# The end of a decode kernel: the last eleven rows of w4 summed on four column groups, the final copy divided between two engines, the output issued by SyncE

## Chip, cores, metric

One core of a Trainium2 chip. The metric is device time in microseconds (us). Each run also has a span, from the first to the last instruction of the program in the record (rounded to 0.1 us), and a granted TensorE clock. Ratios are the mean time of one kernel's fast runs over that of the other's fast runs of the same rounds, so they are not quite the ratio of the medians that are quoted.

## The reference, cut to what matters

```python
xn = layernorm(x)                                    # one token, D = 1024
out = x + attention(layernorm-ed x) @ wo + mixer_mlp(xn)
# attention: 32 query heads, 4 KV heads, 65536 keys of 128: 134 MB of K and V
# mixer_mlp ends in gelu(layernorm(x1) @ w3) @ w4,   w4: 3584 x 1024 (7.3 MB)
# output: 1 x 1 x 1024, bf16
```

About 170 MB pass through the core once, and the result is one row.

## The kernel before

SyncE issues all large loads in one order into three slots of SBUF: wq, w3, w1 and w2, then K and V in 8 MB blocks, wo, and last w4. w4 comes in eight pieces, smaller towards the end, so that little work follows the last byte. The row `psB` in PSUM gathers everything that is added to the output. It lies as two halves of 512 columns on partitions 0 and 32, two column groups of TensorE (matmuls that `tile_position` places so that group j writes from partition 32j on).

```python
W4_PIECES = (6, 5, 6, 4, 3, 2, 1, 1)          # 28 rows of w4

def row_acc(j, lhsT, rhs, start=False):
    nc.tensor.matmul(psB[32 * j:32 * j + lhsT.shape[1], :], lhsT=lhsT, rhs=rhs, start=start, stop=False,
                     tile_position=(0, 32 * j), skip_group_check=True)
# ... cut ...
def compute_w4(lo, hi):
    wt = st.tiles["w4"]
    for c in range(lo, hi):
        for j in range(2):
            row_acc(j, hT[:, c:c + 1], wt[:, D * c + 512 * j:D * c + 512 * (j + 1)])
# ... cut ...
early = sum(W4_PIECES[:2])
compute_w4(0, early)
project(HKV - 1)
compute_w4(early, FC)
out_t = ogpool.tile([64, 512], BF16, name="out_t", tag="og")
nc.scalar.copy(out=out_t[:], in_=psB[0:64, :])
nc.scalar.dma_start(out=out[0, 0, :].rearrange("(j n) -> j n", j=2),
                    in_=out_t[:].rearrange("(a b) n -> a b n", b=32)[:, 0, :])
```

## Time and profile before

402.85 us, median of three runs (402.81 to 403.03).

| part of the end, from the timeline and the chain | us |
|---|---|
| last row of w4 has landed | 397.32 |
| its two matmuls | 397.36, 0.40 long |
| ScalarE copies 64x512 out of PSUM | 397.78, 0.58 long |
| ScalarE's sequencer (the part of an engine that waits and issues DMAs) issues the output DMA | 398.39, 0.58 long |
| end of the span | 400.91 |

Two lines of the page of the kernel before, in 40 equal slices of the span: the busy share of the DMA engines in tenths, and what they moved.

```profile
DMA  9989999999999999999999999999999999999895
GB/s 412 425 366 433 451 425 425 503 425 418 414 419 432 418 497 420 425 418 425 432 433 471 425 425 418 433 432 432 464 420 425 418 445 394 428 481 432 380 418 205
```

The loads never pause until the last slice. So only what follows the last landed byte can be made shorter by a change at the end. The chain that ended last, before (start in us, length in us, what):

```profile
379.92 17.40 DMA big<-in_B_w_dram
397.32 0.04 issue
397.36 0.40 PE psB L179 x2
397.76 0.02 issue
397.78 0.58 ACT out_t L443
```

The timeline of the same stretch (start, length, engine, line, operation; in brackets the idle time and what ended it):

```profile
392.91 1.03 PE L179 MATMUL psB<-big,hT 128*1 128x512 bf16 x8 [0.16 <-DMA big<-in_B_w_dram]
394.81 0.81 PE L179 MATMUL psB<-big,hT 128*1 128x512 bf16 x6 [0.87 <-DMA big<-in_B_w_dram]
397.36 0.38 PE L179 MATMUL psB<-big,hT 128*1 128x512 bf16 x2 [0.26 <-DMA big<-in_B_w_dram]
397.78 0.58 ACT L443 CAST out_t<-psB 64x512 bf16<-64x512 f32 x1 [29.53 <-PE psB L179]
398.39 0.58 ACTq L444 DMA_DIRECT2D out_dram<-out_t  x1
```

TensorE waits for each piece of w4 in turn: it has time to spare until the last one. After the last landing at 397.32 there are 3.59 us in a row without overlap (400.906 - 397.317).

### The profile page before, as it was taken

The numbers are of one execution on the slowest core, as the hardware profiler recorded it, in microseconds if no ns is written. First come the engines' busy times: TensorE is split into PE (matmuls) and PEld (weight loads), VectorE is DVE, ScalarE is ACT, GpSimd is POOL, SyncE is SP. The second block draws the span as 40 slices with busy tenths as digits, with TensorE's granted clock in tenths as the row PEclk, the third lists the DMA queues.
The fourth block names the chain that finished last, engine by engine and source line by source line (L and its number), as shares of the span: only waits on it lengthen the run. The fifth ranks groups of instructions, "written<-read, shape, count | busy, mean of one in ns | idle before, by whom it ended". The sixth has DMA issues, their size and how long they took to land.

```text
span 400.9 us, 2563 instructions
## 1 busy us (share of the span) xinstructions
PE 230.4 (57%) x1348; PEld 44.2 (11%) x854; DVE 209.0 (52%) x154; ACT 27.3 (7%) x35; POOL 5.3 (1%) x28
## 2 busy tenths in 40 slices
PE   0470970591668246922965195629453936594985
PEld 0210000010200110010102010201020002000231
DVE  0511010974196549644953894269349931975040
ACT  1001010003000200020002000100100020002000
POOL 2000000000000000000000000000000000000000
PEclk9995795597679666968796799568866986697999
DMA  9989999999999999999999999999999999999895
GB/s 412 425 366 433 451 425 425 503 425 418 414 419 432 418 497 420 425 418 425 432 433 471 425 425 418 433 432 432 464 420 425 418 445 394 428 481 432 380 418 205
DMA packets 4575, 170.01 MB, mean 424 GB/s; under 512 B 467, under 2 KB 469, under 8 KB 982
## 3 DMA queue, kind: packets, MB, share of 16 engines
q1 hardware_dynamic: 4560, 169.87, 98.4%
q8 instruction: 8, 0.13, 0.1%
q14 instruction: 1, 0.01, 0.0%
q10 hardware_dynamic: 6, 0.00, 0.0%
HBM read 169.87 MB, written 0.00 MB: 424 GB/s over the span
## 4 chain that ended last, share of the span: by engine, by line
DMA 52%; DVE 26%; PE 16%; ACT 3%; another core or an unknown queue 2%; issue 1%; DVEq 0%; ACTq 0%
DMA big<-in_A_k_cache_dram 31%; DVE big L315 19%; DMA big<-in_A_v_cache_dram 10%; PE sc L320 8%; PE oacc L370 6%; DMA big<-in_A_wq_dram 6%; DMA big<-in_B_w_dram 4%; DVE p_sb L341 3%; DVE mx L325 3%; ACT p_sb L338 3%; PE psq L245 1%; PE pm_mx L327 0%; DVE m L329 0%; PE pm_mx L334 0%
## 5 line engine op out<-in xcount | busy, mean ns | idle before, releaser
L320 PE MATMUL sc<-big,qdiag 128*128 128x512 bf16 x512 | 127.7, 409 | 66.4 <-DVE big L315 66.4
L315 DVE STREAM_TRANSPOSE big<-big 128x4096 f32<-128x4096 f32 x32 | 139.4, 4413 | 50.5 <-DMA big<-in_A_k_cache_dram 50.4
L370 PE MATMUL oacc<-big,p_sb 128*32 128x512 bf16 x512 | 44.7, 521 | 34.5 <-DVE p_sb L341 34.5
L325 DVE TENSOR_REDUCE mx<-sc 128x1 f32<-128x2048 f32 x8 | 18.3, 2292 | 29.8 <-PE sc L320 29.8
L320 PEld LDWEIGHTS <-qdiag 128*128 128x128 bf16 x128 | 13.0, 102 | 176.6 <-issue 145.9
L338 ACT ACTIVATE p_sb<-sc,nball 128x2048 bf16<-128x2048 f32 x8 | 15.7, 1967 | 218.7 <-DVE nball L336 218.7
L341 DVE STREAM_TRANSPOSE p_sb<-p_sb 128x2048 bf16<-128x2048 bf16 x8 | 18.5, 2311 | 18.0 <-ACT p_sb L338 18.0
L370 PEld LDWEIGHTS <-p_sb 128*32 128x32 bf16 x512 | 16.6, 126 | 59.4 <-DVE p_sb L341 35.1
L245 PE MATMUL psh<-big,ln_rep_b 128*32 128x512 bf16 (+1 forms) x64 | 12.4, 941 | 8.0 <-DMA big<-in_B_w_dram 8.0
L409 PE MATMUL o_acc<-big,oT 128*1 128x512 bf16 x48 | 12.5, 428 | 2.4 <-ACT p_sb L338 2.4
L327 PE MATMUL pm_mx<-ident_f,mx 128*1 128x128 f32 x8 | 2.3, 283 | 19.1 <-DVE mx L325 19.1
L284 DVE STREAM_TRANSPOSE h_row<-h_row 128x896 bf16<-128x896 bf16 x1 | 1.1, 1111 | 21.1 <-ACT h_row L283 21.1
L379 DVE SCALAR_TENSOR_TENSOR og<-oacc,wb,og 128x512 f32<-128x512 f32 x4 | 3.0, 745 | 15.7 <-PE oacc L370 15.7
L179 PE MATMUL psB<-big,hT 128*1 128x512 bf16 x56 | 7.4, 378 | 1.8 <-DMA big<-in_B_w_dram 1.7
L193 PE MATMUL pm_ln<-ln_rowsum_a,ones_f 128*128 128x1 f32 x2 | 0.6, 347 | 13.3 <-DVE ln_rowsum_a L191 13.3
L415 DVE COPY o_rows<-o_acc 1x1024 f32<-1x1024 f32 x1 | 1.2, 1212 | 13.3 <-PE oacc L370 13.3
L184 DVE STREAM_TRANSPOSE x_t<-x_row 32x256 bf16<-32x256 bf16 x4 | 2.5, 616 | 8.9 <-DMA x_row<-in_A_x_dram 8.9
L269 POOL COPY qdiag<-qx 32x32 bf16<-32x32 bf16 x16 | 3.2, 203 | 279.9 <-PE sc L320 249.7
L391 PE MATMUL pm_e<-ol,sel8big 128*128 128x129 f32 x8 | 2.3, 370 | 8.2 <-DVE ol L390 8.2
L245 PE MATMUL psq<-big,ln_rep_a 128*32 128x512 bf16 x64 | 5.9, 547 | 1.3 <-DMA big<-in_A_wq_dram 1.3
L257 DVE CAST q_row<-psq 128x512 bf16<-128x512 f32 x1 | 0.7, 691 | 7.9 <-PE psq L245 7.9
L334 PE MATMUL pm_mx<-ident_f,rep 1*128 1x1 f32 x8 | 1.9, 241 | 5.0 <-DVE rep L331 5.0
(95 smaller groups left out, 72.6 us busy)
## 6 DMA issues: line engine op xcount, KB each, us to landing
big<-in_A_wo_dram SPq DMA_DIRECT2D x1, 8192.0 KB, 36.7
big<-in_B_w_dram SPq DMA_DIRECT2D x1, 7168.0 KB, 38.5
big<-in_B_w_dram SPq DMA_DIRECT2D x2, 2048.0 KB, 46.4
big<-in_B_w_dram SPq DMA_DIRECT2D x2, 1536.0 KB, 27.3
big<-in_B_w_dram SPq DMA_DIRECT2D x1, 1280.0 KB, 24.1
big<-in_B_w_dram SPq DMA_DIRECT2D x1, 1024.0 KB
big<-in_B_w_dram SPq DMA_DIRECT2D x1, 768.0 KB, 30.8
big<-in_B_w_dram SPq DMA_DIRECT2D x1, 512.0 KB, 31.5
```

The source lines that it names most:

```text
L179: nc.tensor.matmul(psB[32 * j:32 * j + lhsT.shape[1], :], lhsT=lhsT, rhs=rhs, start=start, stop=False, tile_position=(0, 32 * j), skip_gro ...
L184: nc.vector.transpose(out=x_t[32 * a:32 * a + 32].rearrange("p c j -> p (c j)"), in_=x_row[:, 256 * a:256 * (a + 1)].rearrange("p (i c) -> ...
L245: nc.tensor.matmul(acc[32 * q:32 * q + 32, i, 0:n], lhsT=rep[:, c, :], rhs=cols(c, i, q), start=(c == 0), stop=(c == DC - 1), tile_positio ...
L269: nc.gpsimd.tensor_copy(out=qdiag[at, LEAD:].rearrange("p (x c) -> p x c", x=4)[:, :, 32 * a:32 * a + 8], in_=qx[at, :, 8 * g:8 * g + 8])
L315: nc.vector.transpose(out=words, in_=words)
L320: nc.tensor.matmul(sc[:, e, :], lhsT=qdiag[:, c0:c0 + P], rhs=cols[:, s, e, :, b2, :, r], start=(s == 0 and b2 == 0 and r == 0), stop=(s = ...
L325: nc.vector.reduce_max(out=mx[:], in_=sc[:].rearrange("p e n -> p (e n)"), axis=AX.X)
L338: nc.scalar.activation(out=p_sb[:], in_=sc[:], func=ACTF.Exp, bias=nball[:, b:b + 1], scale=SCALE, accum_out=group["lall"][:, b:b + 1])
L341: nc.vector.transpose(out=flat, in_=flat)
L370: nc.tensor.matmul(oacc[32 * q:32 * (q + 1), :], lhsT=pT[:, e, 32 * t:32 * (t + 1)], rhs=vt[:, :, e, t, :], start=(e == 0 and t < 4), stop ...
L379: nc.vector.scalar_tensor_tensor(out=og[:], in0=oacc[:], scalar=wb[:, 1:2], in1=og[:], op0=ALU.mult, op1=ALU.add)
L409: nc.tensor.matmul(tail["rows"][0:1, h2, :], lhsT=oT[g][:, j:j + 1], rhs=wt[:, g, j, 512 * h2:512 * (h2 + 1)], start=(g == 0 and j == 0), ...
```

## The change

The intent is to shorten that row of steps. From row 17 on, w4 is summed on four column groups of 256 columns, in a second PSUM bank. What stood in `psB` by then is folded into it once by matmuls with the identity. The final copy has 256 columns instead of 512 and is shared by ScalarE and VectorE, and SyncE, which has nothing left to do, issues the output.

```diff
+    def compute_w4_quarters(lo, hi, start=False):
+        wt = st.tiles["w4"]
+        for c in range(lo, hi):
+            for q in range(4):
+                nc.tensor.matmul(tail["quarters"][32 * q:32 * q + 1, :], lhsT=hT[:, c:c + 1],
+                                 rhs=wt[:, D * c + 256 * q:D * c + 256 * (q + 1)], start=(start and c == lo),
+                                 stop=(c == FC - 1), tile_position=(0, 32 * q), skip_group_check=True)
+
+    def fold_halves():
+        halves = ppool.tile([64, 512], F32, name="halves", tag="p")
+        nc.vector.tensor_copy(out=halves[:], in_=psB[0:64, :])
+        for q in range(4):
+            j, h = divmod(q, 2)
+            nc.tensor.matmul(tail["quarters"][32 * q:32 * q + 32, :], lhsT=ident_f[0:64, 32 * j:32 * j + 32],
+                             rhs=halves[:, 256 * h:256 * (h + 1)], start=True, stop=False,
+                             tile_position=(0, 32 * q), skip_group_check=True)
 ... cut ...
+    tail["quarters"] = ps_M.tile([P, 256], F32, name="quarters", tag="pm")
     early = sum(W4_PIECES[:2])
+    halved = sum(W4_PIECES[:3])
     compute_w4(0, early)
     project(HKV - 1)
-    compute_w4(early, FC)
-    out_t = ogpool.tile([64, 512], BF16, name="out_t", tag="og")
-    nc.scalar.copy(out=out_t[:], in_=psB[0:64, :])
-    nc.scalar.dma_start(out=out[0, 0, :].rearrange("(j n) -> j n", j=2),
-                        in_=out_t[:].rearrange("(a b) n -> a b n", b=32)[:, 0, :])
+    compute_w4(early, halved)
+    fold_halves()
+    compute_w4_quarters(halved, FC)
+    out_t = ogpool.tile([P, 256], BF16, name="out_t", tag="og")
+    nc.scalar.copy(out=out_t[:, 0:128], in_=tail["quarters"][:, 0:128])
+    nc.vector.tensor_copy(out=out_t[:, 128:256], in_=tail["quarters"][:, 128:256])
+    nc.sync.dma_start(out=out[0, 0, :].rearrange("(j n) -> j n", j=4),
+                      in_=out_t[:].rearrange("(a b) n -> a b n", b=32)[:, 0, :])
```

## The prediction

> **What bounds the kernel now.** The load stream: the page's slices show the DMA engines at 90% or more nearly everywhere, about 424 GB/s, and the chain of waits ends in the w4 load for 17.4 us. Only what follows w4's last byte can be shortened here. By the chain and the timeline of the end (profile span 400.9 us): the last w4 row lands at 397.32; its two 512-column matmuls start at 397.36 and take 0.40 together; the ScalarE copy 64x512 starts at 397.78 and takes 0.58; the ACT-issued output DMA starts at 398.39 and takes 0.58, to 398.97; about 1.9 us of landing and program end follow. So 3.6 us is exposed; 1.6 us of it is touched.
>
> **What changes, costed.**
> 1. Last row: four 256-column matmuls on four column groups instead of two of 512. A 512-column one takes 378 ns, 213 of it streaming at full clock; I estimate 272 ns for 256, with starts some 10 ns apart (three weight loads here overlap within 0.09 us). About 0.31 instead of 0.40: saves 0.09.
> 2. Copies: the ScalarE forms (1014 ns at 1024 columns, 597 at 512, 484 at 384) give about 0.27 us for 128 columns; VectorE's cast from PSUM of the same 128x128 shape takes 0.293. Side by side this would save 0.29. But in the built kernel the VectorE copy waits on ScalarE, not on the matmuls, so I expect them one after the other: 0.27 + 0.04 + 0.29 = 0.60; no saving, 0.02 to 0.05 lost. It fits the Trainium skill, "PSUM — Partial Sum Buffer", section "PSUM bank collisions raise a hardware error": two engines on one bank and quadrant collide, reads against reads too, and both halves lie in one bank. The trace before has no such pair to confirm it.
> 3. Output issue: SyncE's issues take 0.33 to 0.52 us, ACT's 0.52 and 0.58. I take 0.42 for a small one: saves about 0.15. The extra cross-engine hand-over costs 0.02 to 0.05. Landing should not change: the skill's "DMA: Bandwidth & Descriptors", section "Issuing engines are not separate DMA queues", says the issuer saves sequencer time only.
> 4. Added: a VectorE copy 64x512 (0.69 by the like cast) and four fp32 fold matmuls (about 0.6, from the 585 ns passes of the o_rows matmuls, overlapped over column groups) after row 16, about 392.75 to 394.1. Rows 17 to 20 landed at 392.9, so PE falls behind by 1.2 us; at 0.11 to 0.23 us a row it is back before rows 24 and 25 land at 396.07. Off the critical path, with 0.3 us or more to spare.
>
> **On the critical path:** -0.09 (matmuls), +0.03 (copies), -0.15 (issue): about -0.2 us.
>
> **Predicted time: 402.65 us, range 402.2 to 403.1.** Chances: faster by over 2% 0.01, within 2% 0.985, slower by over 2% 0.005.
>
> **What would show it.** The chain still ends in the w4 load; at the end, last matmul group about 0.3 us, ScalarE copy about 0.27, the VectorE copy only after it (idle time put down to ScalarE), SyncE issue near 0.4, span about 400.7. In the waits, PE waits for VectorE's halves about 0.75 us once, and still for DMA at rows 24, 26 and 27.
>
> **What would make it wrong.** The copies running together (0.25 us faster); fold matmuls not overlapping, or 44 weight loads pacing PE at over 0.3 us a row, so the last row finishes late (up to 0.3 us slower); SyncE's issue costing as much as ACT's; a load rate that changes between runs by more than all of this.

## The result

403.19 us, median of four runs (403.15 to 403.67), against 402.86 in the same rounds; ratio 1.0012, 95% interval 0.9998 to 1.0026. The interval touches 1. Still, in these rounds no run of the changed kernel was as fast as the slowest run before (403.03). The expected 0.2 us gain came out as a loss of about 0.33.

The chain that ended last, after:

```profile
394.96 0.69 DVE halves L435
395.66 0.04 issue
395.70 0.64 PE quarters L438 x8
396.34 1.19 PE quarters L429 x40
397.53 0.01 issue
397.54 0.31 PE quarters L429 x4
397.85 0.02 issue
397.87 0.27 ACT out_t L464
398.15 0.02 issue
398.17 0.29 DVE out_t L465
```

and the end of the timeline after:

```profile
397.87 0.27 ACT L464 CAST out_t<-quarters 128x128 bf16<-128x128 f32 x1 [29.48 <-PE quarters L429]
398.17 0.29 DVE L465 CAST out_t<-quarters 128x128 bf16<-128x128 f32 x1 [2.53 <-ACT out_t L464]
398.49 0.64 SPq L466 DMA_DIRECT2D out_dram<-out_t  x1
```

Read against the lines of before, step by step:

- The last matmuls take 0.31 instead of 0.40: gained 0.09, as predicted.
- The copies take 0.27, a hand-over of 0.03, and 0.29, in sequence: 0.59 from 397.87 to 398.46, against 0.58. VectorE's idle time is put down to ScalarE, as predicted.
- The issue takes 0.64 on SyncE against 0.58 on ScalarE. The prediction had 0.42. From the start of the issue to the last landing of the output, the semaphore records give 1.63 us before and 1.65 after.
- From the last landed row to the end of the span: 3.59 before (397.317 to 400.906), 3.53 after (397.501 to 401.027). The whole chain that the change worked on became 0.06 us shorter in this pair of profiles.

So the changed end is a little shorter, and the kernel is slower. Two traces can't explain that: the span of the one is 0.12 us longer than that of the other, and the device time grew by 0.33. The first question is which part of the change carries the loss, the second whether it lies in the span at all.

One more thing differs. The chain after does not go through the load of w4. From 341 us on it stays on the engines, because TensorE was late in this execution: between 380 and 391 us the throttle granted 0.84 of the clock, against 1.00 before. The windows view of before, then after (us from to, length, busy time of PE, PEld, DVE, ACT, POOL, granted clock, DMA share, GB/s):

```profile
380.00:391.00 11.00, 9.41 (x109) 3.54 (x108) 4.54 (x8) 0.00 (x0) 0.00 (x0) 1.00 1.00 419
397.40:397.60 0.20, 0.20 (x2) 0.04 (x1) 0.00 (x0) 0.00 (x0) 0.00 (x0) 1.00 0.00 0
```

```profile
380.00:391.00 11.00, 9.67 (x94) 3.30 (x90) 4.43 (x8) 0.00 (x0) 0.00 (x0) 0.84 1.00 419
397.40:397.60 0.20, 0.19 (x12) 0.06 (x3) 0.00 (x0) 0.00 (x0) 0.00 (x0) 1.00 0.30 82
```

The fold began at 394.96, two microseconds later than I had reckoned, and TensorE finished row 26 at about 397.53, just as the last row landed (397.50, released at 397.54). The spare time had gone to zero, but the last row was not late. The later traces of kernels with the fold agree on the clock: the fold's matmuls, here at 395.70, begin at 395.4 and 395.5 in the two that had 0.84 in this window (e7, e14), and at 393.5 to 393.9 in the three that had 1.00 (e3, e12, e16). The second pair of lines shows something new: 82 GB/s at 397.4, when all of w4's packets have been moved (the last ended at 397.06). It is a fetch of 16 KB of instructions; the page counts nine such packets after, eight before:

```profile
q8 instruction: 8, 0.13, 0.1%
```

```profile
q8 instruction: 9, 0.15, 0.1%
```

### The profile page after: what moved, and what is told of

Read it like the earlier page. It is cut to its first block, busy times and chain, and to the rows that moved or that the text cites. A ratio compares the mean times of both kernels' runs of the same rounds, so it can differ in the third digit from the quotient of the medians.

```text
span 401.0 us, 2625 instructions
## 1 busy us (share of the span) xinstructions
PE 231.5 (58%) x1378; PEld 44.8 (11%) x884; DVE 209.9 (52%) x156; ACT 27.0 (7%) x35; POOL 5.3 (1%) x28
## 4 chain that ended last, share of the span: by engine, by line
DMA 47%; PE 24%; DVE 22%; ACT 3%; another core or an unknown queue 2%; issue 1%; DVEq 0%; ACTq 0%
DMA big<-in_A_k_cache_dram 42%; DVE big L315 15%; PE sc L320 11%; DMA big<-in_A_wq_dram 5%; PE oacc L370 5%; PE o_acc L409 3%; DVE mx L325 3%; ACT p_sb L338 3%; DVE p_sb L341 2%; PE psB L179 2%; PE psq L245 1%; PE pm_mx L327 0%; PE quarters L429 0%; DVE m L329 0%
## 5 line engine op out<-in xcount | busy, mean ns | idle before, releaser
L320 PE MATMUL sc<-big,qdiag 128*128 128x512 bf16 x512 | 129.9, 415 | 66.1 <-DVE big L315 60.6
L370 PE MATMUL oacc<-big,p_sb 128*32 128x512 bf16 x512 | 43.5, 508 | 34.5 <-DVE p_sb L341 34.5
L179 PE MATMUL psB<-big,hT 128*1 128x512 bf16 x34 | 5.4, 468 | 0.0
L376 ACT COPY og<-oacc 128x512 f32<-128x512 f32 x4 | 2.3, 585 | 31.6 <-PE oacc L370 31.6
```

The source lines that it names most:

```text
L320: nc.tensor.matmul(sc[:, e, :], lhsT=qdiag[:, c0:c0 + P], rhs=cols[:, s, e, :, b2, :, r], start=(s == 0 and b2 == 0 and r == 0), stop=(s = ...
L370: nc.tensor.matmul(oacc[32 * q:32 * (q + 1), :], lhsT=pT[:, e, 32 * t:32 * (t + 1)], rhs=vt[:, :, e, t, :], start=(e == 0 and t < 4), stop ...
```

## The experiments

Eighteen kernels ran, in five groups; each group shared nine runs of the kernel before, with medians between 402.76 and 402.89. "Outside" below is device time minus span, averaged over the runs of a kernel. "Landing" is that of the last w4 row, and "tail" is from there to the end of the span; both are from the profiled execution.

### First group: which part carries the loss

The kernel before against itself (no edit).

> The kernel before, run against itself, as the control. Theory 'chance' (the 0.33 us of the changed kernel is a load stream that happened to end later in its executions): this run may differ from the kernel before by as much, 0.2 to 0.4 us. Theory 'real cost' (something the change adds costs 0.3 us every time): this run agrees with the kernel before within 0.1 us, near 402.9. Its profile should again show about 3.59 us from the landing of the last w4 row to the end of the span.

Measured: 402.89 (402.82 to 402.94); tail 3.60; outside 1.78. The landing was at 397.46, against 397.32 in the first profile of the same kernel. So landings scatter by 0.15 us between executions of one kernel, and single device times by a few tenths (402.70 to 403.02 in the nine runs of these rounds); but the medians agree within 0.07. The time outside scatters less: 1.73 to 1.85 in all 45 runs of the kernel before. 'Chance' falls as a reading of 0.33 us.

The output by SyncE, alone:

```diff
-    nc.scalar.dma_start(out=out[0, 0, :].rearrange("(j n) -> j n", j=2),
+    nc.sync.dma_start(out=out[0, 0, :].rearrange("(j n) -> j n", j=2),
```

> The kernel before with one part of the change: the output is issued by SyncE instead of ScalarE. My prediction's term: 0.15 us faster (about 402.7), the issue taking 0.42. Theory from the two traces: the issue of a small output costs as much on SyncE (0.64 there, 0.58 on ScalarE), so no gain from this part: tail from last landing to span's end 3.59 to 3.65, time 402.85 to 402.95. Theory 'the issuer is the real cost': 0.2 to 0.3 us slower, about 403.1 to 403.2.

Measured: 403.27 (403.14 to 403.30) against 402.82, so this one word costs all of the loss. But the tail was 3.57, not longer than before, and the issue took 0.62. The loss lies outside the span: 2.14 us there, against 1.80.

The change with the output back on ScalarE:

```diff
-    nc.sync.dma_start(out=out[0, 0, :].rearrange("(j n) -> j n", j=4),
+    nc.scalar.dma_start(out=out[0, 0, :].rearrange("(j n) -> j n", j=4),
```

> The changed kernel with the output issued by ScalarE again. If the issuer carries the loss: 402.8 to 402.9. If it is the quarters or the program's size: about 403.1 to 403.2, as the changed kernel. Tail from last landing to span's end about 3.5 in both cases (0.31 matmuls, 0.27 and 0.29 copies one after the other).

Measured: 402.77 (402.73 to 403.11); tail 3.55; outside 1.79. All that remains of the change is worth some hundredths of a microsecond. The run of 403.11 is the profiled one. Its timeline has, for the last row:

```profile
397.81 0.28 PE L429 MATMUL quarters<-big,hT 128*1 128x256 bf16 x4 [0.49 <-DMA big<-in_B_w_dram]
```

TensorE waited until 397.81 for the last row. Each of these loads lands in sixteen shares, one for each DMA engine. Fifteen of that row had landed by 397.32, and the sixteenth came at 397.77. The ninth instruction fetch started at 397.21; in the windows view it is the 82 GB/s here:

```profile
396.80:397.00 0.20, 0.00 (x0) 0.00 (x0) 0.00 (x0) 0.00 (x0) 0.00 (x0) 1.00 0.08 31
397.00:397.20 0.20, 0.16 (x4) 0.09 (x4) 0.00 (x0) 0.00 (x0) 0.00 (x0) 1.00 0.06 20
397.20:397.40 0.20, 0.12 (x4) 0.00 (x0) 0.00 (x0) 0.00 (x0) 0.00 (x0) 1.00 0.34 82
397.40:397.60 0.20, 0.00 (x0) 0.00 (x0) 0.00 (x0) 0.00 (x0) 0.00 (x0) 1.00 0.00 0
```

It is tempting to blame the fetch for the late share, but the packet records do not bear that out. The late engine was behind before the fetch: the other fifteen had sent their last packet of w4 by 396.90, and this one, alone at work from 397.00 to 397.20 (DMA share 0.06, one sixteenth), ended at 397.21, just as the fetch began. From last packet to landing its share took 0.57 us, against 0.43 to 0.46 for the five before it (matched in order), so at most some 0.1 us of the 0.45 can be the fetch's. Why the engine was behind is not known. In the profile of the changed kernel the fetch started at 397.42, also after w4's last packet.

The padded kernel: as many more TensorE instructions as the change has, at another place.

```diff
     compute_w12()
+    spare = ps_M.tile([P, 512], F32, name="spare", tag="pm")
+    for i in range(31):
+        q = i % 4
+        nc.tensor.matmul(spare[32 * q:32 * q + 1, 0:64], lhsT=hT[:, i % FC:i % FC + 1], rhs=spread[:, 0, 0:64],
+                         start=True, stop=True, tile_position=(0, 32 * q), skip_group_check=True)
```

> The kernel before with 31 pairs of weight load and small matmul added early, where TensorE waits for loads: about as many more TensorE instructions as the change adds (60), and nothing else. Theory 'program size' (one more 16 KB piece of instructions is fetched, and more before the start): slower by 0.2 to 0.3 us, about 403.1. Any other theory: as the kernel before, 402.9 within 0.1.

Measured: 404.08 (403.90 to 404.36), 1.2 us slower; neither figure was right. Outside was 1.78, so the whole loss lies in the span, and the landing was at 398.69. Windows of the padded kernel:

```profile
395.00:396.00 1.00, 0.00 (x0) 0.00 (x0) 0.00 (x0) 0.00 (x0) 0.00 (x0) 1.00 0.67 248
396.00:397.00 1.00, 0.68 (x6) 0.25 (x6) 0.00 (x0) 0.00 (x0) 0.00 (x0) 1.00 0.39 145
397.00:398.00 1.00, 0.71 (x6) 0.17 (x4) 0.00 (x0) 0.00 (x0) 0.00 (x0) 1.00 0.06 25
398.00:399.00 1.00, 0.67 (x6) 0.16 (x3) 0.00 (x0) 0.00 (x0) 0.00 (x0) 1.00 0.01 4
```

and two of the same stretches before:

```profile
395.00:396.00 1.00, 0.62 (x6) 0.17 (x3) 0.00 (x0) 0.00 (x0) 0.00 (x0) 1.00 0.64 248
397.00:398.00 1.00, 0.48 (x4) 0.08 (x1) 0.00 (x0) 0.22 (x1) 0.00 (x0) 1.00 0.00 0
```

From 397 to 398, 0.06 of the DMA engines' time is used: one engine of sixteen is still at work. The trace has the ninth fetch, 16 KB in one packet of 1.07 us, starting at 394.10. Sixteen packets of the loads were in flight until then, mostly fifteen during the fetch, and from then on one share of each piece lands about 1.3 us after the others. A fetch at 383.44 in the kernel before left no share of the last row late (397.07 to 397.32), so 14 us were enough to make up for it, and four were not. This is one trace; the spans of the other four runs (402.1 to 402.6) are as long. The Trainium skill, "Runtime: NRT & Kernel Launch", section "Instruction fetch mechanics", says that an engine's program is refilled in 16 KiB blocks by its sequencer's own DMA queue and that the cost of crossing a block is "mostly hidden". The size agrees with the packets here. At this place the cost is not hidden.

### Second group: is it the issuer, and what is the divided copy worth

One load more for SyncE, output by ScalarE (`early` is kept at 11 rows by hand):

```diff
-W4_PIECES = (6, 5, 6, 4, 3, 2, 1, 1)
+W4_PIECES = (3, 3, 5, 6, 4, 3, 2, 1, 1)
```

> The kernel before, output still issued by ScalarE, but the first w4 piece loaded in two DMAs: SyncE issues one DMA more, as it does in the changed kernel. The runs so far give a device time minus span of 1.80 us with the output issued by ScalarE and 2.15 us with SyncE. Theory 'SyncE's program is longer by one DMA': 2.15 here, time about 403.2. Theory 'it matters who issues the output': 1.80 here, time about 402.85.

Measured: 402.78 (402.74 to 403.07), outside 1.77.

Output by SyncE, one load less:

```diff
-W4_PIECES = (6, 5, 6, 4, 3, 2, 1, 1)
+W4_PIECES = (11, 6, 4, 3, 2, 1, 1)
```

> Output issued by SyncE, but the first two w4 pieces loaded by one DMA, so SyncE issues as many DMAs in all as in the kernel before. Theory 'SyncE's program is longer by one DMA': device time minus span 1.80, time about 402.85. Theory 'it matters who issues the output': 2.15, time about 403.2.

Measured: 403.22 (403.08 to 403.64), outside 2.11. Both runs speak against the length of SyncE's program and, so far, for the issuer.

The change with the output by ScalarE and one undivided copy:

```diff
-    nc.scalar.copy(out=out_t[:, 0:128], in_=tail["quarters"][:, 0:128])
-    nc.vector.tensor_copy(out=out_t[:, 128:256], in_=tail["quarters"][:, 128:256])
+    nc.scalar.copy(out=out_t[:], in_=tail["quarters"][:])
```

> The changed kernel with the output issued by ScalarE and the final copy done whole by ScalarE (128x256, no VectorE half). Estimate for the copy from the forms at 384 and 512 columns: 0.38 us, against 0.27 and 0.29 one after the other with a hand-over, 0.59. Theory 'the split gains nothing because its halves run in sequence, and loses to one copy': tail from last landing to span's end 3.34, time 402.6. Theory 'the split is worth something': slower than the ScalarE-issued variant of the change (402.77).

Measured: 402.57 (402.52 to 402.62), against 402.89 (402.74 to 402.93) before; ratio 0.9993, interval 0.9981 to 1.0006. The interval holds 1, but the two sets of runs do not overlap. The timeline of its end:

```profile
397.78 0.37 ACT L464 CAST out_t<-quarters 128x256 bf16<-128x256 f32 x1 [29.49 <-PE quarters L429]
398.18 0.61 ACTq L465 DMA_DIRECT2D out_dram<-out_t  x1
```

One copy of 256 columns takes 0.37; the divided one took 0.59. The tail is 3.33, as expected (3.34). The division was what ate the gain of the quarters.

The padded kernel with 12 pairs (`range(31)` to `range(12)`):

> The kernel before padded with 12 instead of 31 pairs of weight load and matmul at the same early place. The padded run lost 1.2 us, and its trace has a ninth 16 KB fetch of instructions at 394.1 us, with one DMA engine's share of the w4 pieces landing 1.3 us after the others. Theory 'the ninth fetch, in the last pieces of the load stream, costs it': with 24 instructions more the ninth fetch is not reached, so 402.8 to 402.9. Theory 'the padding itself costs': about 12/31 of it, 403.3.

Measured: 402.96, with runs of 402.70, 402.90, 402.96, 403.90 and 404.00. My premise was wrong: with 24 instructions more the ninth fetch is reached already, at 396.88 in the profiled execution. There the last row landed at 397.59, which is within the scatter. In the two longest runs the spans are ordinary (401.2 and 400.9) and the microsecond lies outside the span. I can't tell why; this run settles nothing but that the padding alone does not cost in proportion.

### Third group: a theory of DRAM tensors that fell

The runs so far allowed another theory: that each DRAM tensor that an engine's DMAs name costs it something outside the span.

```diff
     st.pump()
+    spare_row = small.tile([1, 32], BF16, name="spare_row")
+    nc.sync.dma_start(out=spare_row[:], in_=B_x[0, 0:1, 0:32])
```

> The kernel before, output still issued by ScalarE, plus one 64-byte load by SyncE from B_x, a tensor that SyncE did not touch before; nothing waits for it but the end. Theory 'per tensor' (each further DRAM tensor that an engine's DMAs name costs that engine about 0.35 us outside the recorded span, and SyncE, with eight tensors, is the longest): device time minus span 2.15, time about 403.2. Theory 'it matters who issues the output, the last DMA': 1.80, time about 402.85.

Measured: 402.56 (402.53 to 402.63), outside 1.79: the theory falls. That it was 0.2 us faster than the kernel before (402.76 in its rounds) was not expected. From the landing of the output to the end of the span it took 0.83 us instead of 0.89; the rest is unexplained. The traces of the other two kernels with one DMA more (e5, e16) show 0.82 there too, that of the one with a DMA less (e6) 0.95, and the rest 0.89.

Output by SyncE, with w1 and w2 loaded by ScalarE:

```diff
-                go(out=t[:, 0:DC * D], in_=B_w1.rearrange("(p c) n -> p (c n)", c=DC))
-                go(out=t[:, DC * D:2 * DC * D], in_=B_w2.rearrange("(m c) n -> m (c n)", c=DC))
+                nc.scalar.dma_start(out=t[:, 0:DC * D], in_=B_w1.rearrange("(p c) n -> p (c n)", c=DC))
+                nc.scalar.dma_start(out=t[:, DC * D:2 * DC * D], in_=B_w2.rearrange("(m c) n -> m (c n)", c=DC))
```

> Output issued by SyncE, but the loads of w1 and w2 issued by ScalarE: SyncE then names seven tensors, the output among them, against eight in the kernel before. Theory 'per tensor': device time minus span 1.45. Theory 'it matters who issues the output': 2.15.

The same edit on the variant with one copy, output by ScalarE:

> The best variant so far (quarters, one ScalarE copy, output issued by ScalarE, 402.57) with the loads of w1 and w2 issued by ScalarE: SyncE names six tensors, ScalarE four. Theory 'per tensor': device time minus span about 1.1, time about 401.9 if the load stream is not disturbed. Otherwise 1.80 and 402.6.

Both were 20 us slower (422.39 and 422.27), because the load stream was disturbed: the first V block was issued at 85.7 us in the first of them, against 52.2 before. What counts here is only the time outside the span: 1.75 with the output by SyncE, 2.08 with the output by ScalarE. The issuer theory had 2.15 and 1.80, the contrary, and the tensor theory 1.45 and 1.1, so both fall.

The change again, unedited:

> The changed kernel again, beside the same runs of the kernel before: 403.15 to 403.25 in most executions, device time minus span 2.15; an execution in which the ninth instruction fetch comes before the last row has landed should be up to 0.5 us longer, with the span longer by as much (one of four was, 403.67).

Measured: 403.33 (403.12 to 403.43) against 402.76, ratio 1.0013, interval 1.0001 to 1.0026; outside 2.17. The loss repeats. What I expected of the fetch failed: it began at 396.85, before the last row had landed (397.48), and no share was late. Nor was one in the trace of e16, with the fetch at 396.72; in those of e7 and e14 (397.24 and 397.15) it began after w4's last packet. In this profile the tail is 3.62, because the four last matmuls took 0.41 together instead of 0.31: the throttle granted half the clock just then. The windows view has it (the granted clock is the third figure from the right):

```profile
397.40:398.00 0.60, 0.38 (x4) 0.09 (x3) 0.00 (x0) 0.04 (x1) 0.00 (x0) 0.50 0.00 0
```

Its chain is of the expected form and comes out of the load of w4:

```profile
380.12 17.36 DMA big<-in_B_w_dram
397.48 0.04 issue
397.52 0.41 PE quarters L429 x4
```

### Fourth and fifth group: the length of ScalarE's program

What goes with the time outside the span in these runs is the number of ScalarE's recorded instructions, those of its sequencer included (waits, issues, drains; counted in the packed trace, since the page counts only the 35 busy ones). Moving the output to SyncE takes two away: the issue and a wait. So two idle instructions were given back:

```diff
     nc.scalar.activation(out=warm_act[:], in_=eps_t[:], func=ACTF.Sqrt)
+    for i in range(2):
+        nc.scalar.copy(out=warm_act[:], in_=eps_t[:])
```

> The kernel before with the output issued by SyncE and two one-column copies added to ScalarE's program near its start, so that it has 57 recorded instructions again instead of 55. Theory 'length of ScalarE's program': device time minus span back at 1.80, time about 402.85. Theory 'issuer': 2.15 and 403.2, as with the output issued by SyncE alone.

Measured: 402.77 (402.73 to 402.89), outside 1.78. SyncE issues the output as in the slow run, and the loss is gone:

```profile
397.87 0.58 ACT L445 CAST out_t<-psB 64x512 bf16<-64x512 f32 x1 [29.52 <-PE psB L181]
398.47 0.61 SPq L446 DMA_DIRECT2D out_dram<-out_t  x1
```

The same two instructions in the changed kernel:

> The changed kernel with the same two one-column copies on ScalarE (57 instructions instead of 55). Theory 'length of ScalarE's program': device time minus span 1.80, time about 402.8, a little under the kernel before. Theory 'issuer': 2.15 and 403.2 to 403.3.

Measured: 402.87 (402.83 to 402.88 in four runs, 403.40 in one) against 402.85; outside about 1.8 in those four, 2.2 in the one. Without the accident of the program's length the change is worth nothing, neither gain nor loss.

The same two in the kernel before:

> The kernel before, output issued by ScalarE, with the two copies added (59 instructions). Theory 'length of ScalarE's program', by the one run that had 59 (2.08): device time minus span 2.1, time about 403.15. Theory 'issuer': 1.80 and 402.85.

Measured: 403.02 (402.99 to 403.12), outside 2.01.

One instruction, then four, in the kernel before (`range(1)`, `range(4)`):

> The kernel before with one one-column copy added on ScalarE: 58 recorded instructions. Theory 'period of four': somewhere between 1.8 and 2.0 outside the span, no firm number. Theory 'only longer or shorter programs than the tuned one lose, step by step': 1.9.

Measured: 402.91 (402.86 to 403.19), outside 1.94, or 1.88 without the one run of five that has 2.2.

> The kernel before with four one-column copies added on ScalarE: 61 recorded instructions. Theory 'period of four instructions': 1.80 outside the span, time about 402.85. Theory 'one good number': 2.0 or more, 403.05 or more.

Measured: 402.80 (402.69 to 402.89), outside 1.78.

| ScalarE's recorded instructions | kernels (issuer of the output) | outside the span, us |
|---|---|---|
| 55 | the change 2.17 and again 2.17, SyncE alone 2.14, SyncE with one load less 2.11 (all SyncE) | 2.11 to 2.17 |
| 57 | before 1.80 (45 runs), e1, e3, e4, e5, e7, e9, e16 (ScalarE); e10, e13 (SyncE) | 1.75 to 1.81 |
| 57 | e14 (SyncE) 1.89, e8 (ScalarE) 2.23 | 1.8 but for one and two runs |
| 58 | before with one more (ScalarE) | 1.94 |
| 59 | e15 2.01, e11 2.08 (ScalarE) | 2.01 to 2.08 |
| 61 | before with four more (ScalarE) | 1.78 |

57 and 61 are good, 55 and 59 bad; 57 is good whoever issues. The 19 runs with 55 lie between 2.08 and 2.27, clear of the 45 of the kernel before (1.73 to 1.85). SyncE's own count does not go with it: it is 61 both in e2 (2.14) and in e13 (1.78). That fits a period of four instructions, but two good numbers do not prove one. What the core does in this time is not in the record: it starts with the program's first instruction and ends with its last. Which side of the span grows, and what waits there, stays open.

### A version that beats both

Quarters, one ScalarE copy, ScalarE's issue, and the 64-byte load of above:

> Quarters with one ScalarE copy and ScalarE issue (402.57 in its run), plus the 64-byte load that came out 0.2 us faster than the kernel before when added alone. If the two add up: 402.35. If that 0.2 was chance: 402.57.

Measured: 402.52 (402.46 to 402.54) against 402.85 (402.68 to 403.18) in the same rounds; ratio 0.9991, interval 0.9979 to 1.0004, no overlap of the runs. The gain of the small load did not add up: 0.05 us by the medians, 0.01 when each is taken against its own rounds, not 0.2. The variant with one copy and without it (402.57) is the plain improvement: 0.3 us, or 0.07%.

## Why the prediction was wrong

The step that failed is the third, the output's issue. The prediction had it 0.15 us shorter on SyncE and, but for a hand-over of 0.02 to 0.05, nothing else touched by it. Measured, the issue was not shorter (0.64 against 0.58, to landing 1.65 against 1.63), and moving it added 0.37 us outside the span. Step by step:

- What bounds the kernel: right. In nearly all profiles the last row waits for the load of w4, and the rest follows in a row.
- Last matmuls, 0.09 saved: right (0.40 to 0.31). The Trainium skill, "TensorE: Matmul & The Clock Gate", section "Measured speedup vs the span model", gives the span of a packed group as one matmul's duration plus 4 ns for each further tile. With the 272 ns of the prediction that is an estimate of 284. The traces agree: 270 ns for one, starts 3 to 4 ns apart, 0.28 for the four at full clock. (The estimate of 272 comes out of the trace before, too: at clock 1.00 rows of 512 columns start 216 ns apart from 389.56 on, so half the columns should take about 108 off 378.)
- Copies in sequence, no saving: right (0.59). It was read from the built kernel, where VectorE's copy waits for ScalarE's. The Trainium skill, "PSUM — Partial Sum Buffer", section "PSUM bank collisions raise a hardware error", says that the compiler's scheduler adds a dependency between two engines' instructions on one bank and quadrant, reads included. No run here tried the two at once, so that page is neither confirmed nor denied. What I did not see is that one undivided copy would have been better: 0.37.
- Output issue, 0.15 saved: wrong. I took 0.42 for a small issue on SyncE, between its 0.33 and 0.52 for large loads. Measured are 0.61 to 0.64, as long as ScalarE's. So this term of the sum is zero: start of issue to landing is 1.60 to 1.67 us on either engine. That agrees with the page "DMA: Bandwidth & Descriptors", section "Issuing engines are not separate DMA queues": whoever starts a DMA, it runs on the same 16 DMA engines.
- Fold off the critical path: right in effect, wrong in size. In the first profile of the change nothing of the 0.3 us of spare time was left, because TensorE ran at a lower clock before; the last row was still not late. The waits for DMA that I expected at rows 24, 26 and 27 were absent in that execution and back in the next one (three, 1.3 us in total).
- Missing from the sum altogether: the time outside the span, +0.37 us (2.17 against 1.80), because the output's issue left ScalarE. This is what turned next to no change into a loss; e13 and e14 show it, by giving two idle instructions back. Why the length of ScalarE's program matters stays open.
- Missing as well: a ninth instruction fetch next to the last landing. In the padded kernel, at 394.10, the one trace puts the 1.2 us down to it. In the kernels with the quarters it came between 396.72 and 397.42, and no trace of theirs shows that it cost more than about 0.1 (e11, with its disturbed stream, had it at 415.10, and its last share came 0.24 after the one before). The cause of the run of 403.67 (span 401.4), of which there is no trace, stays open.

Summed: the tail gives -0.06 in the first profile (with the short matmuls; +0.02 in the second, against 3.60), the time outside +0.37, together +0.31 to +0.39; measured +0.33 by the medians of the first rounds and +0.57 by those of e12. By the means of its nine runs the changed kernel's span is 401.12, against 401.04 of 45 runs before; with the 0.37 outside that is +0.45. The 0.08 of the span has no known cause.

## What to carry to other kernels

Divide a copy out of PSUM between two engines only if the built kernel lets them run together: here 128 + 128 columns in sequence took 0.59 us, and 256 columns on one engine 0.37. Where tenths of a microsecond are at stake, compare device time with the span before looking for the loss in the trace: moving one instruction to another engine (e2) cost 0.34 us outside the span, where no trace shows it. More instructions on an engine whose program is fetched in pieces can put a fetch into the last microseconds of the load stream, so look at the instruction queue's packets there.

## What the Trainium skill lacked or had wrong

- "Runtime: NRT & Kernel Launch", "Instruction fetch mechanics": the cost of crossing a 16 KiB block is called mostly hidden. At the end of a load stream that keeps all sixteen DMA engines busy the padded kernel lost 1.26 us (404.08 against 402.82), with one engine's share of every later piece landing about 1.3 us late. With fetches from 396.72 on, after nearly all of w4 had been moved, nothing of this size was seen.
- The same page has nothing on device time that depends on the length of an engine's program: 55, 57, 58, 59 and 61 recorded ScalarE instructions gave about 2.14, 1.80, 1.94, 2.05 and 1.78 us outside the span.
- "DMA: Bandwidth & Descriptors" gives no duration of the issuing instruction of a small store on trn2. Here an output of 2 KB took 0.58 to 0.61 us to issue on ScalarE and 0.61 to 0.64 on SyncE, longer than SyncE's 128-partition loads (0.33 to 0.42 for most).
- "ScalarE: Activation LUTs", section "What ACT_TABLE_LOAD costs", gives 186 ns + 0.833 ns a column for an ACTIVATE without pointer operands, and no such formula for a copy. The copies from PSUM here, recorded as CAST, took 265, 372 and 580 ns at 128, 256 and 512 columns (the last on 64 partitions), some 30 ns less than the 293, 399 and 612 that would be estimated from it. The ACTIVATEs from PSUM in the trace before took 484 and 597 ns at 384 and 512 columns, 22 and 15 less.
